# Converting float64 weights by a multiplication by 2^-112 and a shift, without the range check

One core of a Trainium2 chip (trn2). The metric is the device time of one execution in microseconds; lower is better. The kernel before takes 794.5 us (median of 6 runs, 793.7 to 795.6).

## The reference

A delta-rule attention block (4 batches, 8 heads, 768 tokens, head dimension 48) feeds a two-layer network with a PReLU between (3072 tokens, 384 to 2048 to 384).

```python
k_n = k / (np.linalg.norm(k, axis=-1, keepdims=True) + 1e-06)
for t in range(S):
    y[:, :, t] = np.einsum('bhd,bhde->bhe', q[:, :, t], state)
    v_old = np.einsum('bhde,bhd->bhe', state, kt)
    state = state + bt[:, :, :, None] * np.einsum('bhd,bhe->bhde', kt, vt - v_old)
# bridge: (B,H,S,D) -> (B*S, H*D)
h = x @ w_in
g = np.maximum(h, 0.0) + alpha * np.minimum(h, 0.0)
return (g @ w_out).astype(np.float32)
```

The kernel receives w_in and w_out as 64-bit floats and turns them into fp32 on the chip. Only this conversion is touched by the change.

## The kernel before

A piece of weights arrives as pairs of 32-bit words. `lo` and `hi` are views of the low and the high words (a stride of two words), `dst` is the fp32 result. There are 12 pieces of 512 columns (w_in) and 16 of 384 (w_out). Before VectorE starts piece i, ScalarE has been handed every piece up to i + 1 (`begin(i + 2)`), and the first six of w_in at once (`begin_in`); VectorE does the rest in two slots, divided by `yield`. A weaving function deals such slots out between those of the other work, so the order on each engine is fixed when the program is built.

```python
def begin(n):
    ...
        nc.scalar.activation(dst.bitcast(U32), lo, ACT.Copy, scale=2.0**-29)   # L192: top 3 bits of lo, rounded
        nc.scalar.square(lo.bitcast(FP32), hi.bitcast(FP32))                   # L194: for the range check

def finish():
    for i in range(count):
        begin(i + 2)
        lo, hi, dst = halves(i)
        high = work.tile([128, W_IN_P], U32, name="high", bufs=1)[...]
        nc.vector.tensor_scalar(                                  # L202
            out=high, in0=hi, scalar1=3, scalar2=0x3FFFFFF8,
            op0=ALU.logical_shift_left, op1=ALU.bitwise_and)
        nc.vector.scalar_tensor_tensor(                           # L206: sign and top bit
            out=hi, in0=hi, scalar=0xC0000000, in1=high,
            op0=ALU.bitwise_and, op1=ALU.bitwise_or)
        yield
        nc.vector.tensor_tensor(                                  # L212: add the low bits
            out=dst.bitcast(U32), in0=hi, in1=dst.bitcast(U32), op=ALU.add)
        nc.vector.scalar_tensor_tensor(                           # L215: small values become 0
            out=dst, in0=lo.bitcast(FP32), scalar=LEAST * LEAST, in1=dst,
            op0=ALU.is_ge, op1=ALU.mult)
        done.append(i)
        ...                     # the stage buffer is free: its next load is issued
        yield
```

The order of the program matters as much (fillers, issued by `busy`, are products on TensorE whose results go unused):

```python
busy(BUSY); begin_in(n_in)
for _ in eliminate(0): pass                       # VectorE alone, TensorE runs fillers
weave((chain(ready(0, masks, 1), pair(0, 1)), ...), (part(conv_in, n), n))      # w_in, first pieces, with fillers
weave((chain(ready(2), pair(2)), ...), (chain(conv_in, part(conv_out, 10)), n),
      (statics(...), ...), (ffn_in(0), IN_PARTS))                               # w_in, rest, and w_out
weave((conv_out, PARTS_OUT - 10), (ffn_in(1), IN_PARTS), (statics(...), ...))   # w_out, rest
...
weave((eliminate(1), HB), (ffn_out(0, True), OUT_PARTS))                        # second elimination
```

Of the kernel before, what the change touches and what calls it, by code (L numbers as in the profile page):

```python
# [23 lines left out]
FP32 = mybir.dt.float32  # L24
U32 = mybir.dt.uint32
S8 = mybir.dt.int8
ALU = mybir.AluOpType
# [3 lines left out]
C = 64  # L31
HB = 32
W_IN_P = 512
LEAST = 3.4332275390625e-05
BUSY = 31
EARLY = 6

# [2 lines left out]
def kernel(  # L40
# [11 lines left out]
    nc = tc.nc  # L52
# [14 lines left out]
    work = ctx.enter_context(tc.tile_pool(name="work", bufs=2))  # L67
# [82 lines left out]
    def weights(pieces, stages, ids, done):  # L150








        count = len(pieces)
        fetched, begun = [], []  # L160

        def words(i):
            w = stages[ids[i]]
            dst, src = pieces[i]
            shape = list(dst.shape)
            n = shape[1] * (shape[2] if len(shape) > 2 else 1)
            w = w[:, 0 : 2 * n]
            if len(shape) > 2:
                return w.rearrange("p (f e) -> p f e", f=shape[1]), n
            return w, n  # L170

        def fetch(n):
            while len(fetched) < min(n, count):
                i = len(fetched)
                assert ids[i] not in ids[len(done) : i]
                nc.sync.dma_start(out=words(i)[0], in_=pieces[i][1].bitcast(U32))
                fetched.append(i)

        def flat(x):
            return x.rearrange("p f d -> p (f d)") if len(x.shape) > 2 else x  # L180

        def halves(i):
            w = flat(words(i)[0]).rearrange("p (e w) -> p e w", w=2)
            return w[:, :, 0], w[:, :, 1], flat(pieces[i][0])

        def begin(n):
            while len(begun) < min(n, count):
                i = len(begun)
                assert i < len(fetched)
                lo, hi, dst = halves(i)  # L190

                nc.scalar.activation(dst.bitcast(U32), lo, ACT.Copy, scale=2.0**-29)  # L192

                nc.scalar.square(lo.bitcast(FP32), hi.bitcast(FP32))  # L194
                begun.append(i)

        def finish():
            for i in range(count):
                begin(i + 2)
                lo, hi, dst = halves(i)  # L200
                high = work.tile([128, W_IN_P], U32, name="high", bufs=1)[:, 0 : words(i)[1]]
                nc.vector.tensor_scalar(  # L202
                    out=high, in0=hi, scalar1=3, scalar2=0x3FFFFFF8,
                    op0=ALU.logical_shift_left, op1=ALU.bitwise_and,
                )
                nc.vector.scalar_tensor_tensor(  # L206
                    out=hi, in0=hi, scalar=0xC0000000, in1=high,
                    op0=ALU.bitwise_and, op1=ALU.bitwise_or,
                )
                yield  # L210

                nc.vector.tensor_tensor(  # L212
                    out=dst.bitcast(U32), in0=hi, in1=dst.bitcast(U32), op=ALU.add
                )
                nc.vector.scalar_tensor_tensor(  # L215
                    out=dst, in0=lo.bitcast(FP32), scalar=LEAST * LEAST, in1=dst,
                    op0=ALU.is_ge, op1=ALU.mult,
                )
                done.append(i)
                n = len(fetched)  # L220
                while n < count and ids[n] not in ids[i + 1 : n]:
                    n += 1
                    fetch(n)
                yield

        return fetch, begin, finish()


# [10 lines left out]
    for t in range(2):  # L239
# [6 lines left out]
        out=ones, in_=ones, compare_op=ALU.is_ge, fill=1.0, base=0,  # L246
# [594 lines left out]
```

## Time and profile before

| | before |
|---|---|
| time, median | 794.5 us |
| span in the profile | 792.7 us |
| TensorE (PE) busy | 755.3 us, 95% |
| VectorE (DVE) busy | 429.4 us, 54%, 1007 instructions |
| ScalarE (ACT) busy | 215.4 us, 27% |
| first g of the feed-forward (L565) | starts at 77.87 us |
| second elimination (L404) | starts at 159.60 us |

The two times at the end of the table serve as marks: g at 78 us opens the stretch in which DVE is full, L404 closes it. Their distance, 81.73 us, is called the stage below. (g is the PReLU's output: ScalarE's rectifier writes `low` from TensorE's product p_ffn, and DVE combines the two. The granted clock, used below, is the share of TensorE's full speed that the profile records for a stretch.)

### The profile page before, as it was taken

What the parts mean: (1) busy time and instruction counts of PE and PEld (TensorE: products, weight loads), DVE (VectorE), ACT (ScalarE), POOL (GpSimd) and SP (SyncE); (2) the same over time, 40 slices, a digit from 0 to 9 for tenths busy, and PEclk for the clock granted to TensorE, in tenths of its full rate; (3) what the DMA queues carried; (4) which work ended last, traced back from release to release, by engine and by line L of the source; (5) the groups of instructions that cost most, each with busy time, mean ns of one, the idle gap of its engine ahead of it and who ended that gap; (6) DMA issues with size and microseconds to landing.
All of it is one profiled execution on the core that took longest, in us unless ns stands there. A gap on an engine that the chain in (4) does not pass through costs nothing.

```text
span 792.7 us, 20343 instructions
## 1 busy us (share of the span) xinstructions
PE 755.3 (95%) x8987; PEld 557.1 (70%) x8987; DVE 429.4 (54%) x1007; ACT 215.4 (27%) x443; POOL 23.3 (3%) x80
## 2 busy tenths in 40 slices
PE   5999888698998999999999999999999999999997
PEld 4457666555787678678678678678677687687684
DVE  6997989995599224596234596223595132122030
ACT  3415546412324123124123123123113122021110
POOL 5000000010000000000000000000000000000000
PEclk9999999999999999999999999999999999999999
DMA  7718453211321122122122121111111110100000
GB/s 154 171 41 223 91 138 82 76 26 32 62 45 34 26 41 42 22 41 42 22 41 41 22 42 31 22 32 32 22 32 31 23 38 3 21 12 2 21 0 21
DMA packets 109417, 37.60 MB, mean 47 GB/s; under 512 B 102625, under 2 KB 105713, under 8 KB 109329
## 3 DMA queue, kind: packets, MB, share of 16 engines
q1 hardware_dynamic: 109296, 36.29, 20.7%
q8 instruction: 71, 1.16, 0.6%
q14 instruction: 18, 0.14, 0.1%
q10 hardware_dynamic: 32, 0.01, 0.0%
HBM read 31.56 MB, written 4.72 MB: 46 GB/s over the span
## 4 chain that ended last, share of the span: by engine, by line
PE 64%; DVE 31%; issue 2%; ACT 2%; POOL 1%; POOLq 0%; DVEq 0%; ACTq 0%
PE p_ffn L584 23%; PE p_ffn L554 20%; DVE block L417 6%; DVE prod L411 6%; PE p_ffn L646 5%; DVE g L565 3%; PE p_one L499 2%; PE p_one L446 2%; PE p_one L513 2%; PE p_big L351 2%; PE p_big L484 2%; PE p_one L457 2%; DVE block L397 1%; DVE turned L422 1%; DVE kk L357 1%
## 5 line engine op out<-in xcount | busy, mean ns | idle before, releaser
L554 PE MATMUL p_ffn<-xt,w_in 128*128 128x256 f32 x1152 | 273.5, 389 | 11.9 <-DVE g L565 6.2
L584 PE MATMUL p_ffn<-w_out,g 128*128 128x384 f32 x768 | 261.1, 492 | 3.9 <-ACT y L492 2.2
L554 PEld LDWEIGHTS p_ffn<-xt,w_in 128*128 128x128 f32 x1152 | 214.9, 192 | 46.3 <-ACT space_out L194 5.8
L584 PEld LDWEIGHTS p_ffn<-w_out,g 128*128 128x128 f32 x768 | 142.5, 191 | 94.3 <-ACT y L492 2.6
L565 DVE SCALAR_TENSOR_TENSOR g<-low,al_t,p_ffn 128x256 f32<-128x256 f32 x192 | 83.4, 476 | 121.2 <-ACT low L562 121.2
L562 ACT ACTIVATE low<-p_ffn 128x512 f32<-128x512 f32 x96 | 56.8, 593 | 106.0 <-PE p_ffn L554 100.8
L411 DVE TENSOR_TENSOR prod<-block 128x30 f32<-128x30 f32 (+9 forms) x180 | 59.4, 330 | 5.6
L417 DVE TENSOR_TENSOR block<-block,prod 128x30 f32<-128x30 f32 (+9 forms) x180 | 59.5, 330 | 5.1
L527 DVE TENSOR_TENSOR y<-y,p_one 128x384 f32<-128x384 f32 x22 | 12.2, 552 | 64.2 <-PE p_one L513 64.2
L449 ACT COPY mid<-p_one 128x256 f32<-128x256 f32 x24 | 8.9, 371 | 102.3 <-PE p_one L446 102.2
L646 PE MATMUL p_ffn<-k_t,ident 128*128 128x512 f32 x76 | 36.3, 625 | 0.0
L590 ACT COPY o_sb<-p_ffn 128x384 f32<-128x384 f32 x24 | 11.5, 478 | 90.6 <-PE p_ffn L584 89.8
L513 PEld LDWEIGHTS p_one<-u,a_t 64*64 64x64 f32 x768 | 24.3, 134 | 12.6 <-issue 8.8
L457 PEld LDWEIGHTS p_one<-diag,mid 64*64 64x64 f32 x768 | 24.3, 135 | 11.1 <-issue 9.4
L487 DVE TENSOR_TENSOR r<-v_raw,p_big 128x384 f32<-128x384 f32 x22 | 11.9, 545 | 36.7 <-PE p_big L484 36.5
L499 PEld LDWEIGHTS p_one<-r,inv 64*64 64x64 f32 x704 | 22.2, 134 | 13.3 <-issue 6.9
L460 DVE TENSOR_TENSOR inv<-diag,p_one 128x256 f32<-128x256 f32 x24 | 10.0, 416 | 35.7 <-PE p_one L457 35.7
L513 PE MATMUL p_one<-u,a_t 64*64 64x48 f32 x768 | 27.2, 220 | 1.3 <-DVE u L501 1.3
L446 PE MATMUL p_one<-diag,kk 64*64 64x32 f32 x768 | 26.4, 220 | 2.1 <-ACT diag L435 2.1
L499 PE MATMUL p_one<-r,inv 64*64 64x48 f32 x704 | 25.0, 220 | 3.3 <-DVE r L487 3.3
L446 PEld LDWEIGHTS p_one<-diag,kk 64*64 64x64 f32 x768 | 24.6, 136 | 3.9 <-ACT diag L435 2.7
L457 PE MATMUL p_one<-diag,mid 64*64 64x32 f32 x768 | 26.9, 220 | 0.0
(101 smaller groups left out, 642.9 us busy)
## 6 DMA issues: line engine op xcount, KB each, us to landing
w_out<-in_moe_w_in_dram SPq DMA_DIRECT2D x12, 512.0 KB, 5.8
kl<-in_k_dram SPq DMA_DIRECT2D x50, 96.0 KB, 3.2
qp<-in_q_dram SPq DMA_DIRECT2D x48, 96.0 KB, 3.0
v_raw<-in_v_dram SPq DMA_DIRECT2D x48, 96.0 KB, 2.8
out_dram<-o_sb SPq DMA_DIRECT2D x48, 96.0 KB, 2.2
ke<-in_k_dram SPq DMA_DIRECT2D x46, 96.0 KB, 3.1
space_out<-in_moe_w_out_dram SPq DMA_DIRECT2D x11, 384.0 KB, 3.6
w_out<-in_moe_w_out_dram SPq DMA_DIRECT2D x5, 384.0 KB, 3.6
```

Source lines behind the costliest of these rows:

```text
L351: nc.tensor.matmul(p[half(t), a, w, g], k_t[n][dims(a), g, half(t)], rhs[n][dims(a), g, half(t)],)
L411: nc.vector.tensor_tensor(out=prod, in0=r[:, 0:j, j : j + 1].to_broadcast([128, j, n]), in1=r[:, j : j + 1, j + 1 : HB].to_broadcast([128, ...
L417: nc.vector.tensor_tensor(out=r[:, 0:j, j + 1 : HB], in0=r[:, 0:j, j + 1 : HB], in1=prod, op=ALU.add)
L446: nc.tensor.matmul(p[half(t), h], kk[n][half(t), h], diag[n % NE][half(t), h, 0:HB])
L457: nc.tensor.matmul(p[half(t), h], mid[n % 2][half(t), h], diag[n % NE][half(t), h, HB:C])
L499: nc.tensor.matmul(p[half(t), h], inv[n % NE][half(t), h], rhs_[n][half(t), h // G, h % G])
L513: nc.tensor.matmul(p[half(t), a, g], a_t[n][half(t), a * G + g], us[n][half(t), a * G + g])
L554: nc.tensor.matmul(p_h[:, i], w_in[:, t, (f + i) * 128 : (f + i + 1) * 128], xt[:, t], start=(t == 0), stop=(t == KT - 1),)
L562: nc.scalar.activation(low, p_h, ACT.Relu, scale=-1.0)
L565: nc.vector.scalar_tensor_tensor(out=g[:, i], in0=low[:, i], scalar=al_t[:, f + i : f + i + 1], in1=p_h[:, i], op0=ALU.mult, op1=ALU.add,)
L584: nc.tensor.matmul(p_o[bp], gs[f // 2][:, f % 2, bp * 128 : (bp + 1) * 128], w_out[:, f], start=(f == 0), stop=(f == FT - 1),)
L646: nc.tensor.matmul(p, ident, k_t[NJ - 1].rearrange("p g i -> p (g i)"))
```

## The change

The intent is to get exponent and mantissa right in one floating-point multiplication. Read as an fp32 number, the high word of a float64 has the sign, eight of the eleven exponent bits, and then the rest; multiplied by 2^-112 its exponent has the fp32 bias, and values too small are meant to become zero by themselves (no run tests such values; the test weights are normal random numbers). A shift by 3 then puts the bits in place (and drops the sign, which is inserted last). The range check and the scratch tile `high` go.

```diff
-                nc.scalar.square(lo.bitcast(FP32), hi.bitcast(FP32))
+                nc.scalar.mul(lo.bitcast(FP32), hi.bitcast(FP32), 2.0**-112)
...
-                high = work.tile([128, W_IN_P], U32, name="high", bufs=1)[:, 0 : words(i)[1]]
                 nc.vector.tensor_scalar(
-                    out=high, in0=hi, scalar1=3, scalar2=0x3FFFFFF8,
-                    op0=ALU.logical_shift_left, op1=ALU.bitwise_and,
-                )
-                nc.vector.scalar_tensor_tensor(
-                    out=hi, in0=hi, scalar=0xC0000000, in1=high,
-                    op0=ALU.bitwise_and, op1=ALU.bitwise_or,
+                    out=lo, in0=lo, scalar1=3, scalar2=None, op0=ALU.logical_shift_left
                 )
-                yield
-
                 nc.vector.tensor_tensor(
-                    out=dst.bitcast(U32), in0=hi, in1=dst.bitcast(U32), op=ALU.add
+                    out=dst.bitcast(U32), in0=lo, in1=dst.bitcast(U32), op=ALU.add
                 )
+                yield
                 nc.vector.scalar_tensor_tensor(
-                    out=dst, in0=lo.bitcast(FP32), scalar=LEAST * LEAST, in1=dst,
-                    op0=ALU.is_ge, op1=ALU.mult,
+                    out=dst.bitcast(U32), in0=hi, scalar=0x80000000, in1=dst.bitcast(U32),
+                    op0=ALU.bitwise_and, op1=ALU.bitwise_or,
                 )
```

More of the change, by code (lines that the diff above doesn't have):

```diff
@@ L33 @@
 W_IN_P = 512
-LEAST = 3.4332275390625e-05
 BUSY = 31
@@ L200, in finish @@
                 lo, hi, dst = halves(i)
-                high = work.tile([128, W_IN_P], U32, name="high", bufs=1)[:, 0 : words(i)[1]]
                 nc.vector.tensor_scalar(
-                    out=high, in0=hi, scalar1=3, scalar2=0x3FFFFFF8,
-                    op0=ALU.logical_shift_left, op1=ALU.bitwise_and,
-                )
-                nc.vector.scalar_tensor_tensor(
-                    out=hi, in0=hi, scalar=0xC0000000, in1=high,
-                    op0=ALU.bitwise_and, op1=ALU.bitwise_or,
+                    out=lo, in0=lo, scalar1=3, scalar2=None, op0=ALU.logical_shift_left
+                )
+                nc.vector.tensor_tensor(
+                    out=dst.bitcast(U32), in0=lo, in1=dst.bitcast(U32), op=ALU.add
                 )
                 yield
-                nc.vector.tensor_tensor(
-                    out=dst.bitcast(U32), in0=hi, in1=dst.bitcast(U32), op=ALU.add
-                )
                 nc.vector.scalar_tensor_tensor(
-                    out=dst, in0=lo.bitcast(FP32), scalar=LEAST * LEAST, in1=dst,
-                    op0=ALU.is_ge, op1=ALU.mult,
+                    out=dst.bitcast(U32), in0=hi, scalar=0x80000000, in1=dst.bitcast(U32),
+                    op0=ALU.bitwise_and, op1=ALU.bitwise_or,
                 )
```

## The prediction

> **What bounds the kernel now.** I read the page's second part first (forty slices of the span), then the chain that ended last, then the groups of instructions with shapes kept apart, then busy time by stretch, and last the engines' timelines.
>
> The slices show where VectorE (DVE) is full and where TensorE (PE) is:
>
> ```profile
> PE   5999888698998999999999999999999999999997
> DVE  6997989995599224596234596223595132122030
> PEclk9999999999999999999999999999999999999999
> ```
>
> One slice is 19.8 us. PE is full nearly everywhere except between about 80 and 160 us, where it falls to 8 and 6, and there DVE stands at 8 to 9. So the kernel as a whole is bound by PE, and only one stage by DVE. The busy time by stretch makes this sharp (length; then busy us of PE, weight load, DVE, ACT, POOL; granted PE clock, DMA share, GB/s):
>
> ```profile
> 52.00:70.00 18.00, 17.76 (x342) 12.10 (x340) 16.47 (x32) 5.77 (x13) 0.00 (x0) 1.00 0.56 150
> 70.00:78.00 8.00, 7.76 (x122) 6.35 (x124) 4.95 (x11) 6.47 (x15) 1.19 (x2) 1.00 1.00 257
> 78.00:96.00 18.00, 15.21 (x316) 12.39 (x305) 16.50 (x37) 8.83 (x19) 1.19 (x2) 1.00 0.46 94
> 96.00:120.00 24.00, 20.07 (x340) 16.00 (x340) 21.55 (x47) 11.77 (x26) 1.33 (x4) 0.93 0.52 145
> 120.00:158.00 38.00, 29.75 (x182) 23.20 (x182) 35.23 (x77) 20.82 (x43) 1.85 (x4) 0.91 0.27 76
> 158.00:186.00 28.00, 25.61 (x78) 14.66 (x78) 25.90 (x78) 3.29 (x10) 2.31 (x7) 1.00 0.17 35
> 186.00:792.00 606.00, 596.71 (x7336) 448.96 (x7336) 267.46 (x635) 140.99 (x287) 4.58 (x21) 1.00 0.14 29
> ```
>
> In 52 to 70 us PE is busy 17.76 of 18 us (it runs filler products woven in by count): PE is the bound. From 78 to 158 us DVE is busy 73.3 of 80 us and PE only 65.0, so DVE is the bound. From 158 to 186 DVE runs the next elimination, one dependent step after another, and PE ends its products 2 us before that ends. After 186 PE is busy 98%. Thus whatever DVE gains between 78 and 158 us should reach the end undiminished: the elimination starts when DVE gets to it, and the rest follows.
>
> The chain that ended last, for 20 to 165 us, says the same by name. From about 78 us its pieces are nearly all DVE (start, duration, what):
>
> ```profile
> 126.51 0.43 DVE w_out L212
> 126.96 0.56 DVE w_out L215
> 127.52 0.29 DVE high L202
> 127.84 0.56 DVE w_out L206
> 128.40 0.78 DVE g L565 x2
> 129.18 0.48 DVE w_out L212
> 129.68 0.56 DVE w_out L215
> 130.24 0.28 DVE high L202
> ```
>
> L202, L206, L212 and L215 are the four DVE instructions that convert one piece of the weights. They stand on the path themselves, end to end.
>
> **What the Trainium skill says.** "VectorE: DVE Perf Modes", section "The perf-mode tier table (the rule you actually need)", gives fp32 tensor_scalar in SBUF two elements a cycle and fp32 tensor_tensor one. The trace agrees for these uint32 operations: from 384 to 512 elements L202 grows by 66 to 69 ns (two per cycle at 0.96 GHz) and L206 by 136 ns (one). The section "What auto-detection actually checks" asks only for one source, both sides in SBUF, and even or equal outer dimensions, not for a dense destination; so I expect the new shift, which writes in place with a stride of two words, to keep L202's time. No run yet shows that form. "ScalarE: Activation LUTs", section "Step-by-step: what each stage is for", says that one element per cycle passes whatever the function; the trace agrees, since L194 (square) takes 678 ns and L192 (copy with a scale) 669 ns at the same size. "TensorE: Matmul & The Clock Gate", "Part 1: The HAM clock gate (the "warmup" mystery)", says idleness throttles PE; the trace agrees: the granted clock is 0.93 and 0.91 in the two stretches with PE waits and 1.00 elsewhere here.
>
> **The change part by part.** The groups concerned (count, busy us, mean ns):
>
> ```profile
> L206 DVE SCALAR_TENSOR_TENSOR w_out<-w_out,high 128x512 uint32<-128x512 uint32 x12 | 8.3, 695 | 0.6
> L206 DVE SCALAR_TENSOR_TENSOR space_out<-space_out,high 128x384 uint32<-128x384 uint32 x11 | 6.2, 559 | 0.5
> L206 DVE SCALAR_TENSOR_TENSOR w_out<-w_out,high 128x384 uint32<-128x384 uint32 x5 | 2.8, 561 | 0.2
> L202 DVE TENSOR_SCALAR high<-w_out 128x512 uint32<-128x512 uint32 x12 | 5.0, 420 | 0.0
> L194 ACT ACTIVATE w_out<-w_out 128x512 f32<-128x512 f32 x12 | 8.1, 678 | 0.4
> ```
>
> There are 12 pieces of 512 columns (w_in) and 16 of 384 (w_out).
>
> 1. ScalarE: a square becomes a multiplication by a constant of the same size. Same count, same order, and by L192 the same time (669 against 678 ns). Zero.
>
> 2. DVE before: shift-and-mask, insert the sign, yield, add, compare-and-multiply. After: shift, add, yield, insert the sign. The shift takes L202's place, the add keeps L212's cost (679 and about 546 ns), the sign insertion is a scalar_tensor_tensor like L206 and L215 (695 against 692 ns). One scalar_tensor_tensor per piece goes: busy time falls by 8.3 + 6.2 + 2.8 = 17.3 us, 28 instructions. The first slot of a piece keeps its cost, the second loses one operation.
>
> 3. What the path loses is start to start, not the duration, as neighbours overlap. When one operation uses the result just before it, the trace shows 0.72 us (L212 at 51.91, L215 at 52.63), and for w_out 0.59 (131.14 to 131.73). The dependent pair in the second slot is what goes, so 0.72 per w_in piece and 0.59 per w_out piece, a little less (0.47) where something else stood between; I take 0.58.
>
> 4. Which pieces are on the path. Pieces 0 to 5 of w_in convert at 50 to 71 us under PE's filler: 6 x 0.72 = 4.3 us freed, worth nothing (PE idle there in all is 0.24 us). At 73.2 DVE waits 1.5 us for ScalarE and at 77.87 another 1.07 us, so what it gained before is lost in these waits. After that piece 7 has its second slot, and 8 to 11 and all of w_out follow: 5 x 0.72 + 16 x 0.58 = 3.6 + 9.3 = **12.9 us** gross.
>
> 5. What takes some back. Stage buffers of w_out are refilled after a piece is done, 3.6 us by the issues. The load that ScalarE awaits at 147.08 delays the rectifier at 148.14, which ends at 148.72, and DVE wants it at 149.14: 0.42 us of slack against 0.59 gained in between, so about 0.2 us is lost. The other such load (133.94) holds the norms at 136.69: slack 1.16 us against 2 x 0.59 gained, just even. ScalarE's small pieces in the loop with DVE stay as they are. Everything else has 1 to 3 us slack (the solve's r at 95.91 needs products that PE ended at 90.8). PE itself has 15 us of idle to give, but not always where DVE gives it: I estimate 1.5 us more lost to g waiting for a freshly finished p_ffn. Net 12.9 - 0.2 - 1.5 = about **11 us**, that is 794.5 - 11 = 783.5.
>
> **Rivals.** (a) **PE becomes the bound** of 78 to 158 us at once. It is busy 65.0 us there, some of it at a clock of 0.91 to 0.93, so about 62 us at full clock (an estimate, busy time times clock). DVE would need 80 - 12.9 = 67 us. They are close enough for collisions, not for a swap. If it did swap, the gain would be perhaps 7 us: 787.5. (b) **The shift loses its double rate** by its strided destination. It would then cost like L206: 0.27 us more per w_in piece and 0.21 per w_out piece on the path, 5 x 0.27 + 16 x 0.21 = 4.7 us back, time about 788. The reading above speaks against it. (c) **The first operation now needs ScalarE's product**, which L202 did not. But L206 overwrote what ScalarE read, so it waited for the same instruction, only 0.4 us later, and ScalarE runs two pieces ahead (piece 8: done 77.4, used 81.3; the tightest, w_out's first: done 98.92, used 100.5). Slack stays above 0.8 us: nothing. (d) **All is hidden**, because PE is 95% busy overall: then 794. Against it speaks the chain, on which these instructions lie. (e) **More than the sum**: PE's wait of 3.26 us at 96.47 shrinks, and the clock stays up afterwards; but DVE paces this stretch, so this can only remove collisions: at best 12.9 us, 781.6, and with the earlier pieces 778.
>
> **Range and chances.** Centre 783.5. The gross sum and 1 us for variation between runs bound it below at 780.5; PE's collisions or a part of (b) put the upper end at 787.5. Faster by over 2% would need under 778.7, a gain of 15.9 us, nearly all of the removed 17.3 us of busy time though six pieces lie under filler: 0.05. Slower by 2%: 0.01. Within 2%: 0.94.
>
> **What will show it.** Right, if DVE busy falls by about 17 us (429.4 to 412) with 28 instructions fewer; if the shift takes about 420 and 352 ns; if ScalarE's multiplication takes 670 ns; if the stretch up to about 78 us does not move, L404 of the second elimination (159.69 in the chain) comes some 11 us earlier, and everything after 186 us keeps that lead within 1 us. Wrong, if the shift takes near 690 ns, if DVE shows new waits for ACT on L565 of several us in all, if PE's idle time of 80 to 158 us stays as large as it is, or if the lead at L404 is lost again before the end.

## The result

The changed kernel takes 782.5 us (median of 6, 780.8 to 784.1) and is correct. Ratios here and below are the mean time of one kernel's fast runs over that of the kernel before in the same rounds, so not quite the ratio of the medians: 0.9849, 95% interval 0.9831 to 0.9867. The gain is clear of noise, though under 2%. In the changed kernel the three DVE lines of the conversion are L199 (shift), L203 (add), L207 (sign); the ScalarE lines are L191 and L192; g is L557 and the elimination's first step L396.

Groups of instructions with shapes apart, kernel after (count, busy us, mean ns, then idle before):

```profile
L203 DVE CUSTOM_DVE_ANT_0 w_in<-w_out,w_in 128x1024 uint16<-128x1024 uint16 x12 | 8.3, 692 | 0.4
L207 DVE SCALAR_TENSOR_TENSOR w_in<-w_out,w_in 128x512 uint32<-128x512 uint32 x12 | 8.1, 678 | 0.1
L207 DVE SCALAR_TENSOR_TENSOR w_out<-space_out,w_out 128x384 uint32<-128x384 uint32 x11 | 6.0, 546 | 0.2
L199 DVE TENSOR_SCALAR w_out<-w_out 128x512 uint32<-128x512 uint32 x12 | 5.0, 418 | 0.0
L199 DVE TENSOR_SCALAR space_out<-space_out 128x384 uint32<-128x384 uint32 x11 | 3.9, 355 | 0.0
L192 ACT ACTIVATE w_out<-w_out 128x512 f32<-128x512 f32 x12 | 8.2, 681 | 0.4
```

The shift takes 418 ns where L202 took 420, in spite of its strided destination, and the multiplication on ScalarE 681 ns where the square took 678. What is gone is one scalar_tensor_tensor per piece.

The conversion of one piece of w_out, and the start of the next, in the changed kernel, from DVE's timeline (start, duration, what):

```profile
122.91 0.36 DVE L199 TENSOR_SCALAR space_out<-space_out 128x384 uint32<-128x384 uint32 x1
123.30 0.56 DVE L203 CUSTOM_DVE_ANT_0 w_out<-space_out,w_out 128x768 uint16<-128x768 uint16 x1
123.89 0.56 DVE L207 SCALAR_TENSOR_TENSOR w_out<-space_out,w_out 128x384 uint32<-128x384 uint32 x1
124.36 0.87 DVE L557 SCALAR_TENSOR_TENSOR g<-low,al_t,p_ffn 128x256 f32<-128x256 f32 x2
125.15 0.36 DVE L199 TENSOR_SCALAR space_out<-space_out 128x384 uint32<-128x384 uint32 x1
```

From one shift to the next 2.24 us pass. The same passage before took 2.83 us:

```profile
130.16 0.35 DVE L202 TENSOR_SCALAR high<-space_out 128x384 uint32<-128x384 uint32 x1
...
132.99 0.35 DVE L202 TENSOR_SCALAR high<-space_out 128x384 uint32<-128x384 uint32 x1
```

The difference is 0.59 us, the start-to-start time of a dependent pair, not the 0.56 us that the removed operation lasted. (For all pieces together, see the ledger of the stage below.)

Busy time by stretch, kernel after (length; then busy us of PE, weight load, DVE, ACT, POOL; clock, DMA share, GB/s). The first three stretches are those shown of before; the last is the whole stage, from 78 us to L396:

```profile
52.00:70.00 18.00, 17.76 (x342) 11.89 (x342) 12.83 (x26) 5.27 (x12) 0.00 (x0) 1.00 0.52 145
70.00:78.00 8.00, 7.76 (x94) 6.37 (x93) 3.90 (x9) 6.47 (x15) 0.81 (x2) 1.00 0.97 254
78.00:96.00 18.00, 17.42 (x398) 14.65 (x398) 16.22 (x38) 11.26 (x24) 1.16 (x4) 1.00 0.60 124
...
78.00:148.10 70.10, 61.67 (x858) 49.62 (x858) 62.71 (x142) 42.62 (x89) 2.99 (x10) 1.00 0.47 118
```

And the kernel before over its whole stage:

```profile
78.00:159.60 81.60, 66.03 (x841) 52.27 (x831) 74.56 (x163) 41.98 (x88) 4.37 (x10) 0.94 0.39 101
```

In 52 to 70 us DVE does 3.6 us less (12.83 against 16.47) and PE stands at the same 17.76: nothing comes of it. In the stage DVE does 11.9 us less (62.71 against 74.56), and the stage is 11.5 us shorter by these cuts. PE's clock rose from 0.94 to 1.00, and its busy time fell by 4.4 us; whether that is a cause or a consequence is asked below.

The two longest of the new waits for ScalarE's rectifier in the stage (DVE's timeline, kernel after; the bracket is idle time before and what ended it):

```profile
131.44 0.87 DVE L557 SCALAR_TENSOR_TENSOR g<-low,al_t,p_ffn 128x256 f32<-128x256 f32 x2 [0.67 <-ACT low L554]
...
139.41 0.87 DVE L557 SCALAR_TENSOR_TENSOR g<-low,al_t,p_ffn 128x256 f32<-128x256 f32 x2 [0.32 <-ACT low L554]
```

### The profile page after: what moved, and what is told of

It is laid out like the page before. It is cut to its first block, busy times and chain, and to the rows that moved or that the text cites. A ratio compares the mean times of both kernels' runs of the same rounds, so it can differ in the third digit from the quotient of the medians.

```text
span 781.5 us, 20316 instructions
## 1 busy us (share of the span) xinstructions
PE 749.2 (96%) x8987; PEld 553.1 (71%) x8987; DVE 412.8 (53%) x979; ACT 215.7 (28%) x443; POOL 21.6 (3%) x80
## 4 chain that ended last, share of the span: by engine, by line
PE 65%; DVE 26%; ACT 3%; DMA 2%; issue 2%; POOL 1%; SPq 0%; POOLq 0%; ACTq 0%; DVEq 0%
PE p_ffn L576 24%; PE p_ffn L546 20%; DVE block L409 5%; DVE prod L403 5%; PE p_ffn L638 5%; DVE g L557 3%; PE p_one L491 2%; PE p_one L505 2%; PE p_one L438 2%; PE p_big L343 2%; PE p_big L476 2%; PE p_one L449 2%; DVE turned L414 1%; DVE block L389 1%; DMA space_out<-in_moe_w_out_dram 1%
## 5 line engine op out<-in xcount | busy, mean ns | idle before, releaser
L546 PE MATMUL p_ffn<-xt,w_in 128*128 128x256 f32 x1152 | 268.8, 385 | 9.9 <-DVE g L557 5.3
L546 PEld LDWEIGHTS p_ffn<-xt,w_in 128*128 128x128 f32 x1152 | 211.9, 190 | 43.3 <-issue 6.9
L557 DVE SCALAR_TENSOR_TENSOR g<-low,al_t,p_ffn 128x256 f32<-128x256 f32 x192 | 83.3, 476 | 122.5 <-ACT low L554 122.5
L638 PE MATMUL p_ffn<-k_t,ident 128*128 128x512 f32 x76 | 36.8, 633 | 0.0
L582 ACT COPY o_sb<-p_ffn 128x384 f32<-128x384 f32 x24 | 11.5, 479 | 90.9 <-PE p_ffn L576 90.9
L479 DVE TENSOR_TENSOR r<-v_raw,p_big 128x384 f32<-128x384 f32 x22 | 11.9, 546 | 37.8 <-PE p_big L476 37.6
L638 PEld LDWEIGHTS p_ffn<-k_t,ident 128*128 128x128 f32 x76 | 14.6, 200 | 16.1 <-issue 15.6
```

Source lines behind the costliest of these rows:

```text
L546: nc.tensor.matmul(p_h[:, i], w_in[:, t, (f + i) * 128 : (f + i + 1) * 128], xt[:, t], start=(t == 0), stop=(t == KT - 1),)
L557: nc.vector.scalar_tensor_tensor(out=g[:, i], in0=low[:, i], scalar=al_t[:, f + i : f + i + 1], in1=p_h[:, i], op0=ALU.mult, op1=ALU.add,)
L638: nc.tensor.matmul(p, ident, k_t[NJ - 1].rearrange("p g i -> p (g i)"))
```

## The experiments

Ten altered kernels (e6_or_space and e9_or_warm combine two alterations, e10_all three), and two repetitions; each was timed in 5 rounds against the kernel before on the same chip. Each has six times, e5_or four. All gave a correct output. Theory A: DVE paces the stage, and the gain is the start-to-start time of the removed instructions that lie in it. Rivals: B, any DVE time counts; C, the gain comes from PE, whose waits had pulled its clock down; D, from a shorter chain of dependent steps; E, the staging transfers had become the bound.

The table has the marks from each profile (one execution each) and the times. The rest is the span less the start of the elimination.

| kernel | ratio (95%) | median us | g at | elimination at | stage us | rest us |
|---|---|---|---|---|---|---|
| before | 1 | 794.5 | 77.87 | 159.60 | 81.73 | 633.1 |
| after | 0.9849 (0.9831 to 0.9867) | 782.5 | 78.37 | 148.10 | 69.73 | 633.4 |
| e1_first7 | 0.9998 (0.9980 to 1.0015) | 794.95 | 77.78 | 159.50 | 81.72 | 633.1 |
| e2_w_in | 0.9964 (0.9943 to 0.9986) | 792.5 | 77.10 | 155.97 | 78.87 | 631.5 |
| e3_w_out | 0.9910 (0.9886 to 0.9933) | 787.1 | 78.00 | 151.39 | 73.39 | 631.6 |
| e4_spare | 0.9967 (0.9950 to 0.9984) | 792.4 | 78.20 | 156.25 | 78.05 | 634.0 |
| e7_clock | 0.9998 (0.9980 to 1.0017) | 794.1 | 77.22 | 159.64 | 82.42 | 631.9 |
| e5_or | 0.9838 (0.9824 to 0.9853) | 782.1 | 78.57 | 145.63 | 67.06 | 635.6 |
| e6_or_space | 0.9813 (0.9783 to 0.9844) | 779.8 | 78.56 | 144.14 | 65.58 | 633.1 |
| e8_space | 0.9847 (0.9807 to 0.9887) | 783.9 | 77.05 | 147.00 | 69.95 | 635.0 |
| e9_or_warm | 0.9858 (0.9821 to 0.9895) | 784.2 | 77.55 | 144.37 | 66.82 | 636.9 |
| e10_all | 0.9861 (0.9825 to 0.9897) | 785.0 | 77.27 | 144.37 | 67.10 | 640.0 |
| e11_after | 0.9837 (0.9800 to 0.9875) | 782.3 | 78.70 | 148.56 | 69.86 | 632.1 |
| e12_again | 0.9785 (0.9744 to 0.9826) | 777.5 | 77.77 | 143.91 | 66.14 | 631.6 |

The stage is the finer measure: two profiles of the changed kernel on two chips give 69.73 and 69.86 us, while the rest, which none of the first experiments touches, varies by some us.

A ledger of the stage shows where its time goes on DVE. Each instruction of DVE's timeline is charged from its start to the start of the next, less the wait that the timeline shows before the next (sums in us):

| kernel | conversion instructions | their start-to-start time | other DVE work | waits | stage |
|---|---|---|---|---|---|
| before | 82 | 42.69 | 34.03 | 5.01 | 81.73 |
| after | 61 | 29.70 | 34.29 | 5.74 | 69.73 |
| e4_spare | 82 | 39.21 | 34.15 | 4.69 | 78.05 |
| e5_or | 41 | 21.86 | 34.43 | 10.77 | 67.06 |
| e6_or_space | 41 | 21.95 | 34.46 | 9.17 | 65.58 |

The conversion gave up 12.99 us, of which 12.00 reached the end of the stage; waits took 0.73 and slightly longer other work 0.26.

### Which pieces count

**e1_first7**: the new way for the first seven pieces of w_in alone.

```diff
+def new(count, i):
+    return count == 12 and i < 7
...
+                if new(count, i):   # multiplication; shift, add; sign
+                else:               # square; four operations as before
```

> Only pieces 0 to 6 of w_in are converted the new way; the other 21 keep the old way. Theory A (only what lies after 78 us on VectorE's path counts): VectorE busy falls by 7 x 0.695 = 4.9 us, time within 1 us of the kernel before (about 794.5), because the waits for ScalarE at 73 and 78 us swallow it. Rival B (any VectorE time counts): 7/21 of 12 us or more, 790.5 or below.

Measured: ratio 0.9998, stage 81.72 us. DVE's busy time did fall, to 424.8 us, by 4.6. Where the freed time went is in the waits. DVE's waits from 50 to 80 us, kernel before (total, times, longest):

```profile
DVE norm L304 <- ACT ksq L302: 1.5, 1, 1.5
DVE g L565 <- ACT low L562: 1.1, 1, 1.1
DVE state L531 <- PE p_big L519: 1.1, 2, 0.7
```

The same for e1_first7:

```profile
DVE state L553 <- PE p_big L541: 2.5, 2, 1.4
DVE norm L326 <- ACT ksq L324: 2.3, 1, 2.3
DVE g L587 <- ACT low L584: 1.8, 1, 1.8
DVE inv L482 <- PE p_one L479: 1.0, 2, 0.6
DVE u L523 <- PE p_one L521: 1.0, 1, 1.0
```

Every one of the waits grew, and two new ones came: DVE waits for engines that it did not hold up. Rival B falls.

**e2_w_in** and **e3_w_out**: the same edit with `count == 12` and with `count == 16`.

> All 12 pieces of w_in new, w_out old. Theory A: pieces 7 to 11 count, 5 x 0.72 = 3.6 us: about 791. Rival B: 12 x 0.72 = 8.6 us: 786. Rival C (the gain comes from the removed idle time of TensorE and its clock, chiefly the wait of 3.3 us at 96 us): most of the gain of the whole change appears here already, 784 to 786.

> All 16 pieces of w_out new, w_in old. Theory A: 16 x 0.58 = 9.3 us less about 1 us for new waits: 786 to 787, and the gains of this run and of the one with w_in alone add up to that of the whole change within 1.5 us. Rival B: 16 x 0.58 less nothing, 785, but then w_in alone gives 8.6, and the two don't add up to the 12 measured. Rival C: only 1 to 3 us here.

Measured: the stage shrinks by 2.86 us with w_in alone and by 8.34 us with w_out alone, together 11.20 against 12.00 for the whole change. By the ratios (times 795 us) it is 2.9 and 7.2, together 10.1 against 12.0; the difference lies within the intervals, each near 1.7 us wide to either side. (The expectation, a sum within 1.5 us, is met by the stage, and missed by the ratios, 1.9 us.) The shares are those of theory A, against C too, which wanted most of the gain where the 3.3 us wait of PE lies, within w_in's part.

### Time of the engine, or length of the chain

**e4_spare**: the changed kernel, with one instruction of the removed kind and size put back, on whose result nothing depends.

```diff
                 yield
+                high = work.tile([128, W_IN_P], U32, name="high", bufs=1)[:, 0 : words(i)[1]]
+                nc.vector.scalar_tensor_tensor(
+                    out=high, in0=hi, scalar=0xC0000000, in1=lo,
+                    op0=ALU.bitwise_and, op1=ALU.bitwise_or,
+                )
                 nc.vector.scalar_tensor_tensor(   # sign, as in the change
```

> The changed kernel with one scalar_tensor_tensor per piece put back into the second slot, of the same size as the removed one, on which nothing depends (its result goes unused; the output stays right). Theory A (occupancy of VectorE): start to start an independent one takes 0.61 us for w_in and 0.48 us for w_out by the trace, so 5 x 0.61 + 16 x 0.48 = 10.7 us come back, less the waits of about 1 us that it hides: 791 to 793. Rival D (the gain came from a shorter chain of dependent steps and waits, not from the engine's time): the time stays at 782 to 785.

Measured: 792.4 us, ratio 0.9967; the stage is 78.05 us, so 8.3 of the 12.0 us came back. The spare instruction costs this much (groups, e4_spare):

```profile
L208 DVE SCALAR_TENSOR_TENSOR high<-w_out 128x512 uint32<-128x512 uint32 x12 | 8.1, 677 | 0.0
L208 DVE SCALAR_TENSOR_TENSOR high<-space_out 128x384 uint32<-128x384 uint32 x11 | 6.0, 544 | 0.0
```

Rival D, no time coming back, falls. The return is somewhat less than the 10.7 less 1 us expected of it, and the ledger says why. The conversion took 9.5 us more than in the changed kernel (39.21 against 29.70), the waits 1.05 less. It is 9.5 and not 10.7 because the spare instruction fills a gap: where addition and sign stood next to each other, 0.59 us apart (123.30 to 123.89 above), the spare one follows the addition after 0.48 and the sign follows it after 0.47, so 0.36 comes back.

The same gap is 3.5 us of the change's own gain. e4_spare has as many conversion instructions in the stage as the kernel before (82), in an order with fewer dependent neighbours, and they take 39.21 instead of 42.69 us. So about a quarter of the 13.0 us came from the spacing of dependent instructions, the rest from one instruction less.

### TensorE's clock

**e7_clock**: the kernel before with four filler products where PE waits for the solve's right side (each product shows as two records in the trace).

```diff
         for i in both:
             through_state(i)
+        busy(warm_up)        # 4, in pair(2) only
         yield
```

> The kernel before with four filler products on TensorE (some 2 us) put after the through-state products of the third and fourth step, where TensorE waits 3.3 us for VectorE and its clock falls afterwards. Nothing on VectorE is changed. Theory A (VectorE paces this stage): TensorE's clock stays higher between 96 and 102 us, the eight products that took 3.65 us take about 2, and the time stays at 794 to 795.5. Rival C (TensorE's clock gave the gain): 1.5 us or more faster, 793 or below.

PE in the kernel before, around the wait (start, duration, what, idle before):

```profile
96.47 1.07 PE L499 MATMUL p_one<-r,inv 64*64 64x48 f32 x29 [3.26 <-DVE r L487]
...
98.01 3.65 PE L554 MATMUL p_ffn<-xt,w_in 128*128 128x256 f32 x8
```

PE in e7_clock:

```profile
91.02 3.67 PE L646 MATMUL p_ffn<-k_t,ident 128*128 128x512 f32 x8 [0.88 <-DVE g L565]
...
98.33 1.99 PE L554 MATMUL p_ffn<-xt,w_in 128*128 128x256 f32 x8
```

The fillers did their work: eight products took 1.99 us in place of 3.65. The clock of the two later stretches in e7_clock, against 0.93 and 0.91 before:

```profile
96.00:120.00 24.00, 20.77 (x344) 16.40 (x343) 21.14 (x46) 11.79 (x25) 0.92 (x2) 0.93 0.55 139
120.00:158.00 38.00, 27.11 (x182) 21.02 (x182) 35.14 (x77) 20.60 (x43) 1.85 (x4) 1.00 0.28 76
```

PE is busy 2.6 us less in 120 to 158 us than in the kernel before (27.11 against 29.75), and yet the elimination starts at 159.64 instead of 159.60 and the time is the same (ratio 0.9998). A faster PE buys nothing in this stage. Rival C falls. That the better clock of the changed kernel follows from its shorter waits is likely, but not shown: in e7_clock the clock also rose in 120 to 126 and in 144 to 150 us, far from the fillers (from 0.72 to 1.00), and fell in 108 to 114 us (from 1.00 to 0.79). (The stage as the table cuts it is longer here because its first mark came earlier, not because its end came later.)

### How much more there is

**e5_or**: two DVE instructions a piece. ScalarE rounds the low word's three bits down instead of to nearest, which makes them at most 7, so shift and `or` fit into one instruction.

```diff
-  nc.scalar.activation(dst.bitcast(U32), lo, ACT.Copy, scale=2.0**-29)
+  nc.scalar.activation(dst.bitcast(U32), lo, ACT.Copy, scale=2.0**-29 * (1 - 2.0**-20), bias=-0.5)
...
-  tensor_scalar (shift); tensor_tensor (add)
+  nc.vector.scalar_tensor_tensor(
+      out=dst.bitcast(U32), in0=lo, scalar=3, in1=dst.bitcast(U32),
+      op0=ALU.logical_shift_left, op1=ALU.bitwise_or)
```

**e6_or_space**: the same with a fourth staging buffer for w_out; **e8_space**: the fourth buffer in the changed kernel.

```diff
-    SPACES = 3
+    SPACES = 4
-    ids = [0, 1, 2, 3, 4, 5, 6, 0, 1, 2, 6, 0, 1, 2, 0, 1]
+    ids = [0, 1, 2, 3, 4, 5, 6, 7, 0, 1, 2, 3, 7, 0, 1, 2]
     # and the tile "upper" moved into a shared work buffer, to make room
```

> The changed kernel with the shift and the addition in one scalar_tensor_tensor (shift, then or), which ScalarE makes possible by rounding the low word's three bits down instead of to nearest; two VectorE instructions per piece instead of three, right within the tolerance. By the rule that held, each piece would give 0.45 us (w_in) and 0.39 us (w_out) on the path: 5 x 0.45 + 16 x 0.39 = 8.5 us gross. Theory A1 (VectorE still paces): 775 to 777. Theory A2 (TensorE, the staging transfers and ScalarE take over now, as TensorE is busy 60.7 of the 69 us of the stage in the changed kernel and two w_out pieces already wait for their transfer): 777.5 to 780.

> The kernel with shift and or, and with four staging buffers for w_out instead of three, so that the loads of the last pieces start earlier. If the transfers are what took over: 1 to 3 us faster than with three buffers, and ScalarE's waits for the transfers of moe_w_out are gone. If TensorE or ScalarE took over: the same time within 1 us.

> The changed kernel with four staging buffers for w_out instead of three (the unused room came from the removed work buffer). In the changed kernel's chain the transfers of moe_w_out hold about 8 us between 124 and 138 us, but VectorE waits only 1.2 us for the rectifier there, 1.0 us more than before. Theory A (VectorE still paces; the transfers cost only those waits): 0 to 1.2 us faster than the changed kernel, 781.3 to 782.5, and the second elimination starts at 147 to 148 us. Rival E (the transfers already bind the changed kernel): 3 us or more faster, 779.5 or below.

Measured: with two instructions a piece the stage shrinks from 69.73 to 67.06 us, by 2.7 us of the 8.5 that the rule promised, and the time, 782.1 us, lies above both expectations. The conversion did give up 7.8 us, but DVE's waits grew by 5.0 (ledger). Here the rule ends. The whole stage in e5_or:

```profile
78.00:145.60 67.60, 61.79 (x860) 50.05 (x859) 55.76 (x122) 42.82 (x90) 3.57 (x10) 1.00 0.49 122
```

DVE does 7.0 us less than in the changed kernel (55.76 against 62.71), PE the same 61.8, now 91% of the stage. Waits in that stage, e5_or:

```profile
DVE g L556 <- ACT low L553: 6.2, 7, 2.2
```

In the changed kernel the same wait is, with the 1.78 us before the first g:

```profile
DVE g L557 <- ACT low L554: 3.0, 4, 1.8
```

So DVE now waits for the rectifier. The rectifier seldom waits for PE: in six of the seven cases it starts right behind other work of ScalarE, in five of them behind the two instructions of a later piece, and only the wait at 124.10 us (0.27 us) follows a wait of the rectifier for PE's products. A loop through ScalarE's fixed order has become the bound; of the three that A2 named, ScalarE stands first. The transfers have a part: with a fourth buffer (e6_or_space) the stage is 65.58 us, 1.5 less, as the waits fall by 1.6 us, and the time is 779.8 us, within the 1 to 3 us expected; of the profile's gain over e5_or, though, 2.5 us lie in the rest (633.1 against 635.6). The fourth buffer alone gives the changed kernel nothing (stage 69.95 against 69.73, ratio 0.9847 against 0.9849), although the chain of the changed kernel names a transfer for 11.5% of the stage: the chain passes through it because the steps follow closely, not because it costs that much. Rival E falls.

The elimination starts 2.5 us earlier in e5_or than in the changed kernel, but the span is only 0.3 us shorter (781.2 against 781.5), and the clock tells where the lead was lost. By the next elimination e5_or is 0.95 us behind (206.89 against 205.94), so 3.4 us are gone; the changed kernel then loses more than e5_or to a late load (see the end of the next part), which evens the spans. After the second elimination PE waits some 2 us for ScalarE in all these kernels; what happens to its clock afterwards differs. Ten us each, 30 to 40 us after the elimination's start, in the kernel after and in e5_or:

```profile
178.10:188.10 10.00, 10.00 (x340) 8.27 (x336) 4.95 (x11) 2.63 (x6) 0.20 (x1) 1.00 0.19 38
```

```profile
175.63:185.63 10.00, 10.00 (x210) 7.61 (x210) 2.75 (x6) 1.86 (x4) 0.20 (x1) 0.70 0.12 24
```

**e9_or_warm** and **e10_all** try fillers there, with three and with four buffers:

```diff
     place(NJ)
+    p = ps_ffn()
+    for _ in range(4):
+        nc.tensor.matmul(p, ident, w_in[:, 0, 0:512])
     between_1(NJ)
```

> The shift-and-or kernel with four filler products on TensorE after the elimination, where TensorE waits about 2.1 us. In the shift-and-or kernel's profile the granted clock then fell to 0.70 for 10 us and 2.5 us of its lead were lost between 170 and 206 us. If that is the cause: 2 us faster than without the fillers, about 780, and a clock near 1.00 there. If not: 782 or above (the fillers themselves fit into the wait).

> Shift and or, four staging buffers and the fillers together. If both effects are real and add: 777 to 778. If the fillers do nothing: as with four buffers alone, 779 to 780.

Measured: 784.2 and 785.0 us, no gain (e10_all missed both of its expectations), and the wait is still there. PE in e9_or_warm (the view starts at 165 us and shows five of the eight filler records):

```profile
164.84 2.31 PE L780 MATMUL p_ffn<-w_in,ident 128*128 128x512 f32 x5
166.98 2.10 PE L575 MATMUL p_ffn<-w_out,g 128*128 128x384 f32 x6
171.09 1.12 PE L437 MATMUL p_one<-diag,kk 64*64 64x32 f32 x32 [2.00 <-ACT diag L426]
```

The fillers ran before the last products of the network, not in the wait, so these two runs failed as tests of the clock; e10_all even shows 0.60 in the ten us after. Whether fillers in the right place would help is left open.

**e11_after** and **e12_again** put the unaltered changed kernel and e6_or_space side by side on one chip.

> The changed kernel once more, unaltered, on the same chip as the next run, for a comparison of like with like and for the spread from chip to chip. Expected: 781 to 784, ratio 0.983 to 0.987.

> The shift-and-or kernel with four staging buffers once more, beside the unaltered changed kernel. If its 779.8 us on the earlier chip were a real gain of the conversion stage: 2 to 4 us faster than the changed kernel here too. If they were the chance of the granted clock after the stage: within 1.5 us of it.

Measured: 782.3 us (0.9837) and 777.5 us (0.9785). Five of the six runs of e12_again lie between 776.9 and 778.1 us, five of e11_after between 781.7 and 782.5; the sixth of each is 785.5 and 786.8, with a lower clock (0.99). So two instructions a piece with a fourth buffer gains about 4 us more on this chip, at the price of rounding the mantissa's last bits down. The stage repeats (65.58 and 66.14 us against 69.73 and 69.86 of the changed kernel), so the stage's gain is no chance of the clock after it; the total is less sure. It is the fastest of all here, but its interval overlaps that of the changed kernel, and its sibling with fillers was slower than both; I count the 4 us of the total as probable, not as shown.

## Why the prediction was right

1. **ScalarE, zero.** Confirmed: 681 against 678 ns, and ScalarE's busy time 215.7 against 215.4 us.

2. **DVE's busy time, 17.3 us less, 28 instructions fewer.** Confirmed: 16.6 us, and 979 instead of 1007. The shift kept the double rate (418 and 355 ns); rival (b) of the prediction did not come.

3. **Start to start instead of duration.** Confirmed: 0.59 us in the timeline of one piece, and 12.99 us over all pieces in the ledger, against the 12.9 predicted. How much of that hangs on dependence the prediction did not ask: e4_spare shows 3.5 us.

4. **Which pieces count.** Confirmed best of all: pieces 0 to 6 gave 0.0 us (e1_first7), pieces 7 to 11 gave 2.9 (predicted 3.6), w_out gave 8.3 (9.3 gross).

5. **What is taken back, 1.7 us.** Too large, and wrong in its makeup; that the net came out near is in part luck. The stage lost 0.99 us. DVE's waits for the rectifier after the first g rose from 0.17 to 1.18 us (0.67, 0.32 and 0.19 us). The prediction booked 1.5 us for g waiting for a freshly finished p_ffn, but in none of the three did the rectifier wait for PE: it started right behind a piece's two instructions on ScalarE. Two of those pieces had waited for their load (0.26 and 0.83 us), yet with a fourth buffer (e8_space), where these waits for loads are gone, g waits 1.32 us all the same. So ScalarE's order cost this. The prediction had also said that the stretch up to 78 us would not move: the first mark came 0.5 us later (78.37 against 77.87), since the 76 filler records on PE took 36.8 instead of 36.3 us. In the other runs this mark lies between 77.05 and 78.70 us.

6. **Rivals.** (a), PE as the bound, did not come: PE's idle time in the stage fell from 15.6 to 8.4 us, and e5_or, with 7 us less of DVE work, met the loop through ScalarE. (c) cost nothing: no shift waits for ScalarE in the stage. (ScalarE is one piece ahead there, not two.) (d), all hidden by a PE that is 95% busy, was wrong for the stage view's reason. (e), more than the sum through the clock, is nothing within the stage (e7_clock); after it, the clock moves the lead, as follows.

The lead of 11.5 us at the elimination arrived as 11.2 us at the end of the profile (792.7 less 781.5), within the 1 us predicted. That is luck: two differences of 1.7 and 2 us cancelled. PE's clock after the elimination, before and after the change:

```profile
183.60:189.60 6.00, 3.90 (x37) 2.48 (x36) 3.91 (x3) 2.93 (x8) 0.00 (x0) 0.78 0.00 0
```

```profile
172.10:178.10 6.00, 3.92 (x64) 2.47 (x64) 3.91 (x3) 2.93 (x8) 0.00 (x0) 1.00 0.00 0
```

So at the next elimination the lead was 13.2 us (205.94 against 219.12). Then the changed kernel waited for a load of v and PE for DVE (DVE, then PE):

```profile
458.41 0.56 DVE L462 TENSOR_TENSOR v_raw<-v_raw,norm 128x384 f32<-128x384 f32 x1 [1.26 <-DMA v_raw<-in_v_dram]
```

```profile
461.25 1.10 PE L546 MATMUL p_ffn<-xt,w_in 128*128 128x256 f32 x4 [1.81 <-DVE g L557]
```

In e11_after, the same kernel, DVE does not wait for a load at this place. The stretch from the second elimination to the next takes 59.5 us in the kernel before, and between 57.8 us (after) and 61.3 us (e5_or) in the twelve profiles without fillers in it: a large part of the scatter of the totals arises here.

Slips in the prediction's working that change nothing: busy time times clock in 78 to 158 us gives 61 us, not 62; 2% under 794.5 is 778.6, not 778.7; the best case with the earlier pieces is 777.3, not 778. Its reading of the clock was loose: PE also waited in 78 to 96 us (busy 15.21 of 18), at a clock of 1.00.

## What to carry to other kernels

An engine with half the busy time of another can still set the pace of one stage: cut the span where the bound changes, and count only the instructions in the stretch where the engine does not wait, with their start-to-start time. When a stage has become shorter, do not book the same price for the next saving before looking at the second busiest engine: here 12.0 of 12.9 us came through the first time and 2.7 of 8.5 the second, because waits for ScalarE and for loads grew. A distance between two marks in the profile separates effects of 1 us that the total time, with its changing clock after the stage, does not.

## What the Trainium skill lacked or had wrong

- "VectorE: DVE Perf Modes", "What auto-detection actually checks": it does not spell out a strided destination; its conditions for the double rate, read as in the prediction, allow one, and the runs agree. An in-place uint32 shift over every second word took 418 ns for 512 elements and 355 for 384, as fast as one with a dense destination (420 and 354).
- "VectorE: DVE Perf Modes", "The DRAIN you can't avoid": it gives no price for an operation whose predecessor made its input, against one that is free. For 384 elements, 0.56 us long, the next one started after 0.59 us when dependent and after 0.47 to 0.48 us when not.
- "ScalarE: Activation LUTs", "What ACT_TABLE_LOAD costs": its 186 ns + 0.833 ns per element gives 613 ns for 512 elements with immediate scale and bias (an estimate from that page; it adds 93 ns for a pointer operand); over every second 32-bit word the kernels before and after show 666 to 681 ns.
- "TensorE: Matmul & The Clock Gate", "HAM oscillation — how this bites in real kernels": its rule names idle gaps above about 3.4 us. Here a wait of 1.77 us of PE (e5_or, before the products that follow the elimination) was followed by ten us at a mean clock of 0.70, and a wait of 2.08 us at the same place of the changed kernel by ten us at 1.00. Shorter gaps than the rule's can go with a fall, and not each time.
